# An induced-set attention with a SwiGLU network behind it: x loaded in whole rows, weights rounded in steps, strips of x in pieces on a fixed slot plan

## The chip, the cores and the metric

The kernel runs on one core of a Trainium2 chip. A core has a matrix engine (PE in the profile, with its weight loads as PEld), a vector engine (DVE), an activation engine (ACT), a general engine (POOL) and a sync engine (SP), on which this kernel issues nearly all of its DMAs in the order of its program. The metric is the device time of one execution in microseconds; lower is better. The kernel before takes 1939.54 us as the median of three runs (1937.98 to 1940.28).

## The reference

`x` is 4 batches x 12416 tokens x 128 channels, `inducing` is 32 x 128. Each batch is attended twice, and every token then goes through a gated network of width 1536:

```python
def mab(q, kv):
    s = scale * (q @ kv.transpose(0, 2, 1))
    s = s - s.max(-1, keepdims=True)
    a = np.exp(s)
    a /= a.sum(-1, keepdims=True) + 1e-09
    return a @ kv
h = mab(I, x)                # 32 inducing rows look at 12416 tokens
x = mab(x, h)                # 12416 tokens look at the 32 rows of h
rms = np.sqrt(np.mean(x * x, axis=-1, keepdims=True) + 1e-06)
xn = x / rms * rms_g
g = xn @ w_gate              # 128 -> 1536
silu = g * (1.0 / (1.0 + np.exp(-g)))
val = xn @ w_val
return (silu * val @ w_out).astype(np.float32)
```

The weights arrive as 64-bit floats and must be rounded to 32 bits on the chip; `x` is 32-bit.

## The kernel before, in words

**Tiling.** The 12416 tokens of a batch are cut into seven strips (`per` = 16, 16, 16, 16, 16, 15 and 2 tiles of 128 tokens). A strip is held in two forms: `xn`, by rows, with the tokens on the partitions, and `xT`, with the channels on them. A strip's tokens lie in four groups `q` of 32 partitions. The network works on 25 units per batch: each full strip gives four (one for each `q`), the last strip one. A unit has twelve steps `j`, one for each 128 of the width 1536; a step is called a slot here, so a batch has 300 slots, numbered 12 x unit + j.

**A slot** (`ffn`, L421). PE multiplies the stacked weights `sg` and `sv` (they hold h, the gain and w_gate or w_val together, in a high and a low half) with the unit's gathered attention weights `a` (L441, L443), ACT takes the silu (L445), DVE the product `u` (L447), and PE projects `u` with `wo` into `acc` (L431). Two or three projects are kept back in the list `late`, so PE has work while a new product is made; before the two long ACT steps (`marks`) up to five. After a unit's last project DVE transposes `acc` and SP writes it out in four DMAs (L434 to L437). In slot 2 of each unit SP is given the gather of the next unit's `a` (L417): four DMAs between partitions, for the unit of a smaller strip sixteen.

**Attention for the next batch** goes on between the slots. The steps in order: `turn_x` makes `xT` channel-wise (for batch 0 on PE with a copy on ACT or DVE, later by DVE in place, L225), `scores1` (L249), the maximum over all tokens (`max1` to `max3`), `exp1` (L273), `turn_e` and `sum_h` for h (L277, L285), `end_h`, `turn_h`, `square_h`, then `scores2` and `sub_max` per strip (L322, L330), and `exp2` (L336). `fetch(i)` reads the three rounded weight tiles back from memory (L342), and `stack(i)` multiplies them with h (L351) and lays the result into `sg` or `sv` with twelve DMAs (L358). Before, these steps are spread evenly over slots 0 to 240 of the batch ahead; `fetch(1)` follows right behind `stack(0)`. Each `sum_h` of a strip is followed by the four row loads of the batch after it (L112), and each `scores2` by the four strip loads (L118), all on SP.

**The seam** (`seam`, L369) turns a strip's attention weights into the scaled halves `hi` and `lo` that the gathers read: transposes, a square with the Gram matrix of h for the root mean square, a power on POOL, and the split (L404, L405) into halves, of which there is one buffer.

**The opening** does all of batch 0's attention before the first slot. Its rows come in 28 loads of 32 partitions, on SP and ACT in turn, and nine raw weight chunks of 512 KB are read on SP (L169) and rounded by seven DVE and two POOL operations each (L190 to L199); six are written back to memory (L203) for the later batches. At its end SP holds, in this order: the gather of unit 0, the two stacks, the strips of batch 1 once more (they were already loaded behind `scores2`), and only then the gather of unit 1.

**Buffers and queues.** At most eight DMAs are under way: each waits until the one eight places before it has landed. The pool `wp` of fetched weight tiles has three buffers, `work` three, `halves` one, `astk` (the gathered `a`) three, `up` (the products) seven.

Of the kernel before, what the change touches and what calls it, by code (L numbers as in the profile page):

```python
# [24 lines left out]
def kernel(  # L25
# [9 lines left out]
):  # L35

# [71 lines left out]
    def load_rows(b, s, queues):  # L108
        n = per[s]
        t = xnat[b, s] = xnp.tile([P, n, C], F32, name=f"xn{s}")  # L110
        for q in range(R):
            queues[q % len(queues)].dma_start(out=t[ts(q, m), :, :], in_=of(xrows, b, s)[:, ts(q, n), :])  # L112

    def load_channels(b, s):
        w = R * per[s]
        t = xT[b, s] = xtp.tile([P, w * m], F32, name=f"xT{s}")
        for k in range(R):
            nc.sync.dma_start(out=t[ts(k, m), :].rearrange("p (w c) -> p w c", c=m),  # L118
                              in_=of(xrows, b, s)[:, :, ts(k, m)])

    load_rows(0, 0, [nc.sync, nc.scalar])
# [4 lines left out]
    for s in range(1, NS):  # L126
        load_rows(0, s, [nc.sync, nc.scalar])
# [46 lines left out]
    def load_w(i, c):  # L174
# [7 lines left out]
        if wide:  # L182
            words = raw[i, c].rearrange("p (f w) -> p f w", w=2)
            low, high = words[:, :, 0], words[:, :, 1]
            e, s = (up.tile([P, 512], I32, name="u") for _ in range(2))
            f = astk.tile([P, 512], F32, name="a")
            r = outp.tile([P, 512], F32, name="o")
            fi = f.bitcast(I32)
            ve = nc.vector
            ve.tensor_scalar(out=e[:], in0=high, scalar1=20, scalar2=0x7FF, op0=ALU.logical_shift_right, op1=ALU.bitwise_and)  # L190
            ve.tensor_scalar(out=e[:], in0=e[:], scalar1=896.0, scalar2=1151.0, op0=ALU.max, op1=ALU.min)
            ve.tensor_scalar(out=e[:], in0=e[:], scalar1=-896.0, scalar2=float(1 << 23), op0=ALU.add, op1=ALU.mult)
            ve.tensor_scalar(out=s[:], in0=high, scalar1=-(1 << 31), scalar2=0x3F800000, op0=ALU.bitwise_and, op1=ALU.bitwise_or)
            ve.tensor_scalar(out=fi[:], in0=high, scalar1=12, scalar2=9, op0=ALU.logical_shift_left, op1=ALU.logical_shift_right)  # L194
            ve.tensor_tensor(out=fi[:], in0=fi[:], in1=s[:], op=ALU.bitwise_or)
            ve.scalar_tensor_tensor(out=r[:], in0=low.bitcast(U32), scalar=2.0 ** -52, in1=s.bitcast(F32)[:],  # L196
                                    op0=ALU.mult, op1=ALU.mult)
            nc.gpsimd.tensor_tensor(out=f[:], in0=f[:], in1=r[:], op=ALU.add)  # L198
            nc.gpsimd.tensor_tensor(out=dst, in0=f[:], in1=e.bitcast(F32)[:], op=ALU.mult)  # L199
        else:  # L200
            nc.sync.dma_start(out=dst if i < 2 else dst.rearrange("p (j c) -> p j c", c=C), in_=source(i, c))
        if i < 2:
            nc.sync.dma_start(out=w32[i][c][:], in_=dst)  # L203
# [3 lines left out]
    def attention(b, load_next):  # L207
# [12 lines left out]
        def turn_x(s, k):  # L220
# [9 lines left out]
            if now:  # L230
# [5 lines left out]
                if k % 4 == 3:  # L236
                    nc.vector.tensor_copy(out=dst, in_=src)
                else:
                    nc.scalar.copy(out=dst, in_=src)  # L239
# [39 lines left out]
        def sum_h(s):  # L279
# [11 lines left out]
            if load_next:  # L291
                load_rows(b + 1, s, [nc.sync])
# [53 lines left out]
        def stack(i):  # L346
# [7 lines left out]
            nc.vector.tensor_copy(out=hi[rows, :], in_=ps[rows, :])  # L354
# [262 lines left out]
```

## Time and profile before

| | us |
|---|---|
| median of three runs | 1939.54 |
| the profiled execution's own time | 1944.83 |
| its span, first to last instruction | 1943.1 |
| start of exp1 of batch 0 | 51.81 |
| first gate product of unit 0 | 157.14 |
| first gate product of unit 1 | 212.69 |
| PE busy over the span | 1722.7 |

All sums are made in the span of the profiled execution, which starts at 0. A timeline row gives start, length, engine, line, operation, the tiles written and read, and in brackets how long the engine had been idle and what ended that. "x28" at a row's end says that 28 like instructions in a row are shown as one. SPq is SP's DMA queue. The mean granted clock of PE is 0.953 of the full one.

### The profile page before, as it was taken

How to read it: one execution, taken by the hardware profiler on the slowest of the kernel's cores; microseconds unless marked ns; L12 is line 12 of the kernel's file. 1: busy time of each engine (PE TensorE's matmuls, PEld its weight loads, DVE VectorE, ACT ScalarE, POOL GpSimd, SP SyncE). 2: the span in 40 equal slices, each digit the busy share in tenths (PEclk: the TensorE clock that was granted, in tenths of full speed). 3: DMA queues.
4: the chain of work that ended last, by engine and by line, in shares of the span. 5: the costliest groups of instructions: out<-in, count | busy, mean ns of one | idle time of the engine just before them, and what ended most of it. 6: DMA issues, size and time to landing. Idle time of an engine off the chain costs nothing.

```text
span 1943.1 us, 20398 instructions
## 1 busy us (share of the span) xinstructions
PE 1722.7 (89%) x6258; PEld 959.7 (49%) x6258; DVE 1156.7 (60%) x2010; ACT 751.2 (39%) x1246; POOL 176.9 (9%) x137
## 2 busy tenths in 40 slices
PE   4413699999897999999989899999999899999998
PEld 3201355555454655555545555555555555555555
DVE  1824476666555667566646577666666465656654
ACT  2001244433343443533344344443354344444443
POOL 0321101101101001101101011001011011001100
PEclk9756799999999999999989899999999899999999
DMA  7797411165721111155741111111221111111111
GB/s 186 170 167 126 72 31 29 36 142 104 142 43 29 30 33 33 28 116 109 139 73 32 24 31 33 38 23 44 63 45 33 24 31 33 33 33 33 33 32 26
DMA packets 443197, 120.41 MB, mean 62 GB/s; under 512 B 418736, under 2 KB 422864, under 8 KB 440528
## 3 DMA queue, kind: packets, MB, share of 16 engines
q1 hardware_dynamic: 442224, 115.91, 30.3%
q10 hardware_dynamic: 864, 3.20, 0.7%
q8 instruction: 50, 0.82, 0.2%
q14 instruction: 59, 0.48, 0.1%
HBM read 60.31 MB, written 27.00 MB: 45 GB/s over the span
## 4 chain that ended last, share of the span: by engine, by line
PE 80%; SPq 9%; DMA 5%; ACT 2%; DVE 2%; issue 1%; DVEq 0%; ACTq 0%
PE acc L431 48%; PE gv L441 13%; PE gv L443 13%; SPq L118 5%; SPq L417 3%; DMA xn<-in_x_dram 2%; PE mm L245 2%; DMA a<-lo 1%; PE mm L285 1%; DVE u L447 1%; PE mm L385 1%; PE gv L233 1%; ACT silu L445 1%; SPq L358 0%; SPq L436 0%
## 5 line engine op out<-in xcount | busy, mean ns | idle before, releaser
L431 PE MATMUL acc<-u,wo 128*128 128x512 f32 (+2 forms) x2400 | 1212.9, 588 | 62.3 <-DVE u L447 62.2
L447 DVE TENSOR_TENSOR u<-silu,gv 128x512 f32<-128x512 f32 (+2 forms) x1200 | 796.9, 670 | 598.5 <-ACT silu L445 590.5
L445 ACT ACTIVATE silu<-gv 128x512 f32<-128x512 f32 (+2 forms) x1200 | 700.2, 585 | 1080.1 <-PE gv L441 590.5
L441 PE MATMUL gv<-a,sg 128*128 128x512 f32 (+2 forms) x1200 | 929.9, 775 | 83.7 <-DVE a L194 49.5
L431 PEld LDWEIGHTS acc<-u,wo 128*128 128x128 f32 x2400 | 443.2, 190 | 217.8 <-DVE u L447 77.9
L443 PE MATMUL gv<-a,sv 128*128 128x512 f32 (+2 forms) x1200 | 469.0, 391 | 10.0 <-DMA sv<-wlo 6.7
L441 PEld LDWEIGHTS gv<-a,sg 128*128 128x128 f32 x1200 | 229.0, 191 | 367.0 <-issue 294.6
L443 PEld LDWEIGHTS gv<-a,sv 128*128 128x128 f32 x1200 | 229.8, 191 | 284.6 <-issue 195.6
L388 POOL TENSOR_TENSOR z<-z,sc 128x512 f32<-128x512 f32 (+2 forms) x28 | 31.8, 1136 | 1276.5 <-DVE z L387 1134.6
L396 POOL TENSOR_TENSOR rs<-ms,mhalf 128x16 f32<-128x16 f32 (+2 forms) x28 | 71.8, 2564 | 97.2 <-DVE ms L394 97.1
L434 DVE STREAM_TRANSPOSE o<-acc 128x512 f32<-128x512 f32 (+2 forms) x100 | 69.2, 692 | 1.6 <-PE acc L431 1.1
L225 DVE STREAM_TRANSPOSE xT<-xT 128x512 f32<-128x512 f32 (+2 forms) x84 | 53.2, 633 | 0.0
L404 DVE CAST hi<-aT 128x512 fp32r<-128x512 f32 (+2 forms) x28 | 11.0, 392 | 69.4 <-DMA a<-hi 69.3
L331 POOL TENSOR_TENSOR sc<-sc,mx 128x512 f32<-128x512 f32 (+2 forms) x24 | 22.5, 936 | 220.6 <-ACT silu L445 114.2
L336 ACT ACTIVATE sc<-sc 128x3104 f32<-128x3104 f32 (+2 forms) x5 | 11.4, 2274 | 55.7 <-POOL sc L331 34.5
L233 PE MATMUL gv<-ident,xn 128*128 128x128 f32 x97 | 15.8, 326 | 17.1 <-ACT xT L239 16.4
L385 PE MATMUL mm<-eT,gram 128*128 128x512 f32 (+2 forms) x56 | 26.0, 545 | 0.5 <-DVE eT L376 0.5
L398 POOL TENSOR_TENSOR sc<-sc,rs 128x512 f32<-128x512 f32 (+2 forms) x28 | 26.1, 933 | 2.2
L355 DVE TENSOR_TENSOR wlo<-gv,whi 96x512 fp32r<-96x512 f32 x2 | 1.4, 686 | 39.8 <-DMA sg<-whi 39.8
L233 PEld LDWEIGHTS gv<-ident,xn 128*128 128x128 f32 x97 | 13.4, 169 | 22.9 <-ACT xT L239 20.1
L405 DVE TENSOR_TENSOR lo<-aT,hi 128x512 fp32r<-128x512 f32 (+2 forms) x28 | 17.4, 621 | 11.6 <-DMA a<-lo 11.3
L198 POOL TENSOR_TENSOR a<-a,o 128x512 f32<-128x512 f32 x9 | 11.7, 1303 | 119.0 <-DVE o L196 119.0
(122 smaller groups left out, 466.5 us busy)
## 6 DMA issues: line engine op xcount, KB each, us to landing
xT<-in_x_dram SPq DMA_DIRECT2D x80, 256.0 KB, 5.1
out_dram<-o SPq DMA_DIRECT2D x320, 64.0 KB, 2.0
xn<-in_x_dram SPq DMA_DIRECT2D x70, 256.0 KB, 5.4
a<-hi SPq DMA_DIRECT2D x160, 64.0 KB, 2.0
a<-lo SPq DMA_DIRECT2D x160, 64.0 KB, 2.0
w<-w SPq DMA_DIRECT2D x21, 256.0 KB, 3.1
xT<-in_x_dram SPq DMA_DIRECT2D x16, 240.0 KB, 4.8
out_dram<-o SPq DMA_DIRECT2D x64, 60.0 KB, 2.0
```

Source lines behind the costliest of these rows:

```text
L118: nc.sync.dma_start(out=t[ts(k, m), :].rearrange("p (w c) -> p w c", c=m), in_=of(xrows, b, s)[:, :, ts(k, m)])
L225: nc.vector.transpose(out=t[:, ts(k, n * m)], in_=t[:, ts(k, n * m)])
L233: nc.tensor.transpose(ps[:, ts(t - k * R, P)], xnat[b, s][:, t, :], ident[:])
L385: nc.tensor.matmul(ps[:, 0:n * m], gram[b][:], st["eT"][:], start=True, stop=True)
L396: nc.gpsimd.tensor_tensor(out=rs[:, 0:n], in0=ms[:, 0:n], in1=mhalf[:, 0:n], op=ALU.pow)
L417: nc.sync.dma_start(out=a[ts(k, m), ts(q, w)].bitcast(F32), in_=half[ts(q0 + q, m), 0:w].bitcast(F32))
L431: nc.tensor.matmul(acc[:, 0:T], wo[:, j, :], t[:, 0:T], start=(j == 0), stop=(j == NJ - 1))
L434: nc.vector.transpose(out=o[:, 0:T], in_=acc[:, 0:T])
L441: nc.tensor.matmul(g[:, 0:T], sg[:, ts(j, P)], a[:, 0:T], start=True, stop=True)
L443: nc.tensor.matmul(v[:, 0:T], sv[:, ts(j, P)], a[:, 0:T], start=True, stop=True)
L445: nc.scalar.activation(sl[:, 0:T], g[:, 0:T], AF.Silu)
L447: nc.vector.tensor_tensor(out=t[:, 0:T], in0=sl[:, 0:T], in1=v[:, 0:T], op=ALU.mult)
```

## The change

It does six things.

1. Batch 0's rows come in seven loads of 128 partitions, a strip each, all on SP, with the first three raw weight chunks in between; in this batch a strip's tokens lie in the order (q i t) instead of (i q t), in the output too. ACT makes all the copies into `xT`.
2. The rounding of a chunk is cut into six steps, which are called between other steps: three after each `scores1`, six after `exp1`, six after `square_h`, six inside the first seam, twelve after the gather of unit 0, and the rest in slots 0 to 3. The scaling of the exponent moves from DVE to POOL, except for chunk (1, 2), which is rounded on DVE alone. A new raw chunk is read after one has been put away.
3. `scores2` no longer loads strips. The strips of batch 1 are loaded once: four pieces (one of 32 channels each) at the end of the opening, the others one in every fourth slot. Those of batches 2 and 3 come one in every sixth slot, from slot 215 of the batch before.
4. In batch 0, `scores2` and `sub_max` of strips 1 to 6 and the rest of `exp2` move from the opening into slots 1 to 22.
5. The even spread is replaced by fixed slots: `turn_x` from 20, `scores1` from 36, the maximum at 126 to 130, `exp1` at 134, `turn_e` and `sum_h` from 140, `fetch(0)` at 170, `fetch(1)` at 178, `end_h` at 184, `stack(0)` at 191, `scores2` from 194, `stack(1)` at 198, `exp2` at 254.
6. Each group q is written out by itself, so the last unit of a batch has sixteen small output DMAs instead of four. In the first seam of batch 0 two POOL multiplications are on DVE; the second seam is a unit later; batch 0's `stack` casts on ACT.

The core of the diff:

```diff
     def of(dram, b, s):
-        return dram[ds(b * N + start[s], P * per[s]), :].rearrange("(i w) c -> i w c", i=m)
+        d = dram[ds(b * N + start[s], P * per[s]), :]
+        return d.rearrange("(i q t) c -> q i t c" if b else "(q i t) c -> q i t c", q=R, i=m)
...
-    def load_rows(b, s, queues):
+    def load_rows(b, s):
         n = per[s]
         t = xnat[b, s] = xnp.tile([P, n, C], F32, name=f"xn{s}")
-        for q in range(R):
-            queues[q % len(queues)].dma_start(out=t[ts(q, m), :, :], in_=of(xrows, b, s)[:, ts(q, n), :])
+        if b:
+            for q in range(R):
+                nc.sync.dma_start(out=t[ts(q, m), :, :], in_=of(xrows, b, s)[q])
+        else:
+            nc.sync.dma_start(out=t[:], in_=xrows[ds(start[s], P * n), :].rearrange("(p t) c -> p t c", t=n))
...
+        ge = ve if (i, c) == (1, NC - 1) else nc.gpsimd
+        return [
+            lambda: ve.tensor_scalar(out=e[:], in0=high, scalar1=20, scalar2=0x7FF,
+                                     op0=ALU.logical_shift_right, op1=ALU.bitwise_and),
...
         def scores2(s):
             nc.vector.transpose(out=sc[b][:, cols[s]], in_=scores(s, st["hT"][:, 0:m]))
-            if load_next:
-                load_channels(b + 1, s)
...
-                for k in range(R):
-                    nc.sync.dma_start(out=of(out, b, s)[:, ds(q0 * per[s], nb), ts(k, m)],
-                                      in_=o[ts(k, m), 0:T].rearrange("p (w c) -> p w c", c=m))
+                w = per[s] * m
+                for q in range(nq):
+                    for k in range(R):
+                        nc.sync.dma_start(out=of(out, b, s)[q0 + q][:, :, ts(k, m)],
+                                          in_=o[ts(k, m), ts(q, w)].rearrange("p (t c) -> p t c", c=m))
...
+    for s in range(NS):
+        load_rows(0, s)
+        if reads and s < NC:
+            fetch_raw(*reads.pop(0))
...
         if s:
             f["scores1"](s - 1)
+            convert(6 * NC // (NS - 1))
...
-    convert()
-    convert()
+    convert(6)
...
+    f["fetch"](0)
+    convert(6)
+    turn_a, square, scale, apply, split = seam(0, 0)
+    turn_a()
+    f["stack"](0)
+    square()
+    convert(3)
+    scale()
+    convert(3)
+    f["fetch"](1)
+    f["stack"](1)
+    apply()
+    split()
     gather(0, 0)
-    for i in range(2):
-        f["fetch"](i)
-        f["stack"](i)
-    while queue:
-        convert()
+    convert(12)
+    pieces = {b: [(b, s, k) for s in range(NS) for k in range(R)] for b in range(1, B)}
     if B > 1:
-        for s in range(NS):
-            load_channels(1, s)
+        for _ in range(R):
+            load_channels(*pieces[1].pop(0))
...
+        if not b:
+            for k in range(4):
+                add(k, convert, 3)
+            for s in range(1, NS):
+                add(3 * s - 2, f["scores2"], s)
+                add(3 * s, f["sub_max"], s)
+            add(3 * NS + 1, f["exp2"], 1, NS)
+            marks.append(3 * NS + 1)
+        if b + 1 < B:
+            g = attention(b + 1, b + 2 < B)
+            for k, one in enumerate(pieces[b + 1]):
+                add(4 * k if not b else 6 * k, load_channels, *one)
...
+                add(140 + 6 * s, g["turn_e"], s)
+                add(144 + 6 * s, g["sum_h"], s)
+                add(194 + 8 * s, g["scores2"], s)
...
+            for i in range(2):
+                add(170 + 8 * i, g["fetch"], i)
+                add(191 + 7 * i, g["stack"], i)
+            add(254, g["exp2"], 0, NS)
+            marks += [134, 254]
+        if b + 2 < B:
+            for k in range(215, NU * NJ, 6):
+                add(k, load_channels, *pieces[b + 2].pop(0))
```

Below are two places in SP's order. The first is the end of the opening. Names: `xT` are strips and `xn` rows of batch 1, `w` with a source is a rounded chunk on its way to memory, `a` is the gather, `sg` and `sv` are the stacks. Before:

```order
L118 DMA xT_733<-in_x_dram 32x64x32 x4
L203 DMA w_155<-silu 128x512
L118 DMA xT_762<-in_x_dram 32x60x32 x4
L118 DMA xT_783<-in_x_dram 32x8x32 x4
L417 DMA a<-hi 32x512
L417 DMA a<-lo 32x512
...
L358 DMA sg<-whi 32x512 x6
L358 DMA sg<-wlo 32x512 x6
L358 DMA sv<-whi 32x512 x6
L358 DMA sv<-wlo 32x512 x6
L118 DMA xT_882<-in_x_dram 32x64x32 x4
L118 DMA xT_887<-in_x_dram 32x64x32 x4
```

After:

```order
L115 DMA xn_586<-in_x_dram 32x1920 x4
L115 DMA xn_595<-in_x_dram 32x256 x4
L188 DMA w_119<-silu 128x512
L371 DMA sg<-whi 32x512 x6
L371 DMA sg<-wlo 32x512 x6
L188 DMA w_120<-silu 128x512
L371 DMA sv<-whi 32x512 x6
L371 DMA sv<-wlo 32x512 x6
L434 DMA a<-hi 32x512
L434 DMA a<-lo 32x512
...
L124 DMA xT_758<-in_x_dram 32x64x32 x4
```

The strips ahead of the gather and those behind the stacks are gone but for four pieces; the row loads stand directly ahead of the stacks, and the gather of unit 0 has moved behind them.

The second place is SP around the second weight fetch in a later batch's attention, with the semaphores that each DMA waits for (DMAHW is a DMA eight places before; PE, DVE an engine). Names: `w_...` from `w1...` is the second fetch, `a_...` the gather. After:

```order
L352 DMA w_2871<-w02_117 128x512 [waits DMAHW2_49]
L434 DMA a_2875<-hi_2249 32x512 [waits DMAHW3_49]
...
L115 DMA xn5_2939<-in_x_dram 32x1920 [waits DMAHW7_49,PE_49]
...
L352 DMA w_2982<-w10_118 128x512 [waits DMAHW3_49,PE_49]
L352 DMA w_2983<-w11_119 128x512 [waits DMAHW4_49,PE_49]
L352 DMA w_2984<-w12_120 128x512 [waits DMAHW5_49,PE_49]
L115 DMA xn6_3011<-in_x_dram 32x256 [waits DMAHW6_49]
...
L455 DMA out_0_dram<-o_3026 512x1x32 [waits DMAHW2_49,DVE_49]
...
L434 DMA a_3040<-hi_2900 32x512 [waits DMAHW6_49]
...
L371 DMA sg_3096<-whi_3153 32x512 [waits DMAHW2_49,DVE_49]
```

Before, the second fetch:

```order
L358 DMA sg_2987<-whi_3367 32x512 [waits DMAHW0_49,DVE_49]
...
L358 DMA sg_2987<-wlo_3368 32x512 [waits DMAHW6_49,DVE_49]
...
L342 DMA w_3411<-w10_153 128x512 [waits DMAHW4_49,PE_49]
...
L436 DMA out_0_dram<-o_3418 32x16x32 [waits DMAHW7_49,DVE_49]
...
L417 DMA a_3438<-hi_3000 32x512 [waits DMAHW3_49]
```

On PE, the product that frees the first fetch's tiles stands in the change at slot 191, and the gate product of the next unit, which reads the gather `a_3040`, two places behind it:

```order
L361 MATMUL mm_3149<-w_2869,hg_3092 32x512 [waits DMAHW0_49]
L361 MATMUL mm_3149<-w_2870,hg_3092 32x512 [waits DMAHW1_49]
L361 MATMUL mm_3149<-w_2871,hg_3092 32x512 [waits DMAHW2_49]
L448 MATMUL acc_2998<-u_3129,wo_112 128x512
L460 MATMUL gv_3171<-a_3040,sg_615 128x512 [waits DMAHW6_49,DMAHW1_49,DMAHW7_49,DMAHW0_49,Activation_49]
```

The second fetch now stands ahead of the stack DMAs of the first product, with four small row loads, an output and a gather between them; before, it stood behind them.

More of the change, by code (lines that the diff above doesn't have):

```diff
@@ L454, with convert @@
     f = attention(0, B > 1)
[L455 to L464 removed]
+    reads = chunks[:len(places)]
+    unread = chunks[len(places):]
+    for s in range(NS):
+        load_rows(0, s)
+        if reads and s < NC:
+            fetch_raw(*reads.pop(0))
+    for one in reads:
+        fetch_raw(*one)
+    queue, steps = list(chunks), []
+    def convert(n):
+        for _ in range(n):
+            if not steps and queue:
+                steps.extend(load_w(*queue.pop(0)))
+            if steps:
+                steps.pop(0)()
     f["open_"]()
@@ L487 @@
     f["square_h"]()
-    chain = seam(0, 0)
-    for s in range(1, NS):
-        f["scores2"](s)
-        f["sub_max"](s)
-        if s % 2 and chain:
-            chain.pop(0)()
-        if len(queue) > NC:
-            convert()
-    for k in chain:
-        k()
-    f["exp2"](1, NS)
-    while len(queue) > NC:
-        convert()
-    gather(0, 0)
-    for i in range(2):
-        f["fetch"](i)
-        f["stack"](i)
-    while queue:
-        convert()
+    f["fetch"](0)
+    convert(6)
+    turn_a, square, scale, apply, split = seam(0, 0)
@@ L543, in schedule, with add @@
-        last = units.index((full - 1, 0, 1)) * NJ
-        at = [last * k // len(steps) for k in range(len(steps))]
-        plan = {}
-        for k, step in zip(at, steps):
-            plan.setdefault(k, []).append(step)
-        return plan, [at[k] for k in marks]
+        plan, marks = {}, []
+        def add(k, step, *args):
+            plan.setdefault(int(k), []).append(lambda: step(*args))
+        if not b:
[6 more added lines that the diff above has]
+            marks.append(3 * NS + 1)
```

141 lines of the change are left out of this document (59 added, 82 removed).

## The prediction

> **What bounds the kernel now.** I read the page first, its chain of waits and its 40 slices:
>
> ```profile
> PE 80%; SPq 9%; DMA 5%; ACT 2%; DVE 2%; issue 1%; DVEq 0%; ACTq 0%
> PE   4413699999897999999989899999999899999998
> ```
>
> PE carries 80% of the chain, but SP's queue and the DMAs carry 14%. The slices show where: PE is 40% busy or less in the first four (49 us each), and nearly full afterwards. So the opening is bound by transfers, the rest by PE. The windows from the second unit of batch 0 to the end put numbers on the rest (columns: window, length, busy of PE, PEld, DVE, ACT, POOL, granted clock, DMA share, GB/s):
>
> ```profile
> 213.50:647.30 433.80, 411.30 (x1493) 226.06 (x1493) 270.24 (x474) 178.68 (x295) 38.05 (x28) 0.98 0.34 66
> 647.30:1096.90 449.60, 426.89 (x1541) 235.39 (x1541) 280.45 (x490) 185.85 (x307) 38.01 (x28) 0.98 0.33 64
> 1096.90:1534.10 437.20, 423.69 (x1541) 233.95 (x1541) 280.50 (x490) 185.88 (x308) 38.03 (x28) 0.99 0.18 37
> 1534.10:1943.10 409.00, 393.50 (x1215) 226.97 (x1213) 240.01 (x392) 175.35 (x300) 27.15 (x18) 0.99 0.17 31
> ```
>
> PE idles 22.5, 22.7, 13.5 and 15.5 us in them (length less busy). The gain has to come from the 213 us ahead of them, and a loss from new idle time in them.
>
> **Part 1, to the first softmax.** The windows and the opening's timeline (start, length, engine, line; the last two rows are the page's DMA issues, with KB and us to landing):
>
> ```profile
> 0.00:30.00 30.00, 5.00 (x21) 4.17 (x21) 2.05 (x10) 0.14 (x1) 0.76 (x7) 1.00 0.96 210
> 32.00:36.00 4.00, 4.00 (x20) 2.42 (x19) 0.69 (x1) 2.29 (x5) 0.00 (x0) 1.00 1.03 394
> 64.00:93.00 29.00, 17.41 (x211) 8.14 (x203) 23.54 (x49) 0.63 (x1) 8.58 (x8) 0.79 1.01 231
> 29.86 1.28 ACT L239 ACT_TABLE_LOAD   x1 [29.86 <-DMA xn<-in_x_dram]
> 39.14 1.97 PE L233 MATMUL gv<-ident,xn 128*128 128x128 f32 x16
> 42.03 1.97 PE L233 MATMUL gv<-ident,xn 128*128 128x128 f32 x16
> 51.81 2.88 ACT L273 ACTIVATE sc<-sc,nbias 128x3104 f32<-128x3104 f32 x1 [3.25 <-DVE nbias L269]
> 52.14 0.43 DVE L191 TENSOR_SCALAR u<-u 128x512 int32<-128x512 int32 x1
> 55.40 1.37 DVE L191 TENSOR_SCALAR u<-u 128x512 int32<-128x512 int32 x1
> w<-w SPq DMA_DIRECT2D x21, 256.0 KB, 3.1
> a<-lo SPq DMA_DIRECT2D x160, 64.0 KB, 2.0
> ```
>
> Batch 0's x (6.36 MB) moves at 210 GB/s with the DMA engines 96% busy: 32 partitions per load set that rate, and the same form gives 231 again at 64 to 93. Raw weights into 128 partitions move at 394. ACT issues half the loads and cannot copy before 29.86. Afterwards x and three raw chunks (1.57 MB) come in 128-partition loads: 7.93 MB at 394 GB/s is 20.1 us, and about 3 until the last lands (the `w<-w` row), so 23. A strip costs PE and ACT 2.89 us (39.14 to 42.03); two are left when the last lands, 5.8. The rounding steps put between the scores delay DVE by up to 3 x 0.94 = 2.8 (the same step took 0.43 once and 1.37 three us later); the chain of the maximum takes 2. So exp1 starts at 34, not 51.81. Bounds: 28 if neither strips nor rounding lag (23 + 2.9 + 2), 49 if the loads stay at 210 (37.8 + 3 + the same tail).
>
> The Trainium skill ("DMA: Bandwidth & Descriptors", section "Where 436 GB/s comes from") lets HBM give a core about 358 GB/s; by that the loads would take 22.2 us and the sum be 2 us longer, an estimate by that page. The trace's 394 GB/s, over 4 us only, disagrees.
>
> **Part 2, from there to the second unit.**
>
> ```profile
> 57.91 0.33 SPq L203 DMA_DIRECT2D w<-w  x1
> 60.94 8.88 PE L285 MATMUL gv<-xn,e 128*32 128x128 f32 x194 [9.36 <-DVE e L277]
> 63.76 29.23 SPq L112 DMA_DIRECT2D xn<-in_x_dram  x28
> 93.82 14.18 SPq L118 DMA_DIRECT2D xT<-in_x_dram  x8
> 149.16 3.71 SPq L358 DMA_DIRECT2D sg<-whi  x6
> 157.14 0.76 PE L441 MATMUL gv<-a,sg 128*128 128x512 f32 x1 [49.46 <-DVE a L194]
> 164.32 44.35 SPq L118 DMA_DIRECT2D xT<-in_x_dram  x28
> 210.63 0.59 SPq L417 DMA_DIRECT2D a<-lo  x1
> 212.69 0.76 PE L441 MATMUL gv<-a,sg 128*128 128x512 f32 x1 [28.60 <-DMA a<-lo]
> ```
>
> SP is the path from 63.76 on: 28 row loads for batch 1 (29.23), then 28 strip loads among the spills (93.82 to 146), gather and 24 stack copies (4 x 3.71), then the same 28 strips once more (44.35), behind which unit 1's gather stands. That gather ends unit 0 at 212.69, though its own work is some 20 us. The change takes both sets of strips off this queue; four pieces stay. What stays is SP's 28 row loads, since each strip's rows are replaced as sum_h frees them.
>
> One rounded chunk instead of two stands between exp1 and turn_e, so the first row load comes 7.5 us after exp1's start instead of 12: at 41.5. Then 29.2 of row loads, 3 until the eighth DMA back has landed, 14.8 for the stacks, 1 for two spills (0.33 each if nothing holds them), 2.5 for the gather and 2 for its landing: the first gate at 94, not 157.14. DVE's work in that time (three chunks' steps at 0.4 to 1.4 us, scores2 of strip 0, the seam) lets the first stack be ready at about 62 and the second at 72 to 75; SP comes to them at 74 and 82. So it is hidden, with some 7 us to spare; DVE being later than that would add the difference.
>
> Unit 0 now also holds four of the scores2 steps and the last rounding. The chain in the steady state prices a slot and a block of scores (start, us, what):
>
> ```profile
> 495.52 0.99 PE mm L351 x6
> 499.35 0.86 PE acc L431 x2
> 500.67 0.86 PE acc L431 x2
> 504.62 0.99 PE mm L245 x8
> 552.37 2.70 ACT sc L336
> ```
>
> A slot is 500.67 - 499.35 = 1.32. Twelve are 15.8, four scores 4.0, and I allow 4 for the low clock at the start and DVE's queue: 24. Unit 1 starts at 118 instead of 212.69: **-95 us** (bounds: 28 or 49 for exp1 and 20 or 28 for the unit give -105 and -76).
>
> **Part 3, the steady state.** Its stalls before, in batch 0's seventeenth to twenty-third units:
>
> ```profile
> 516.42 12.53 SPq L118 DMA_DIRECT2D xT<-in_x_dram  x8
> 535.43 0.41 DVE L404 CAST hi<-aT 128x480 fp32r<-128x480 f32 x1 [9.83 <-DMA a<-hi]
> 537.41 2.07 PE L431 MATMUL acc<-u,wo 128*128 128x512 f32 x2 [9.11 <-DVE u L447]
> 630.30 1.97 PE L431 MATMUL acc<-u,wo 128*128 128x480 f32 x2 [8.97 <-DVE u L447]
> 640.63 1.94 SPq L436 DMA_DIRECT2D out_dram<-o  x4
> 646.81 0.47 PE L441 MATMUL gv<-a,sg 128*128 128x512 f32 x1 [0.26 <-DMA a<-lo]
> 509.36 2.11 SPq L342 DMA_DIRECT2D w<-w  x3
> 1930.52 10.08 SPq L436 DMA_DIRECT2D out_dram<-o  x8
> ```
>
> Eight strips in one go (12.53) hold back a gather; DVE's split waits for it 9.83 and PE 9.11. The same happens in batch 1, not in batch 2, which loads no strips. With one strip in four or six slots (1.57 us of SP in 5 to 8) I let both go: -9 each. The stall of 8.97 is of another kind (sixteen small gathers of one unit, then the split that waits for them), and stays.
>
> **The new wait.** The weight tiles have three buffers. Before, the second weight fetch stood behind the first stack product; now it is issued at slot 178 and can't start before the product of slot 191 frees the tiles. SP works in order: behind it stand four small row loads, an output of four DMAs, and the gather of the unit that starts at slot 192. From the product on, SP needs 2.1 (three fetches) + 1.5 (four row loads of 32 KB, by the shortest issue, 0.33, a little over) + 1.9 (output) + 2.4 (four gathers at 0.59) + 2.0 of landing = 9.9, while PE has two stack products and one project left, 1.7. PE so stands **8.2** at the start of that unit in batches 0 and 1, and 6.7 in batch 2, which has no row loads. Floor 0 if the tiles come free earlier than the order says, ceiling 13 if the stalled SP also holds the next gather.
>
> Other terms: two scores2 in unit 1 of batch 0, 2 x 0.99, less what fills gaps: +1.4; exp2 among the units takes ACT away for 2.7 and two table loads of 1.28, of which the queue of ready products covers a part: +3.5. Sixteen output DMAs instead of four at the end of each batch (12 x 0.485, from 1.94 for four): at the end of batches 0 to 2 they delay the next batch's second gather by 5.8, of which about 5 is covered: +1 each in batches 1 to 3; at the very end they stand bare: +5.8.
>
> Sum: -95; batch 0 -9 + 1.4 + 3.5 + 8.2 = +4; batch 1 -9 + 8.2 + 1 = 0; batch 2 6.7 + 1 = +8; batch 3 1 + 5.8 = +7. Net **-75** (-95 + 19, rounded). The profiled execution, 1944.83 us with a span of 1943.1, would come to 1869 with a span of 1867. It lies 5.3 above the median of the runs, 1939.54, so the median comes to **1864**.
>
> **Rivals.** (a) The fetch's wait costs nothing, because gathers are needed later than I count. For it: before, a gather that landed at the last moment cost PE only 0.26 (646.81), so a little slack more would do. Against: the order on SP and the three tiles leave no slack, since product, fetch and gather follow each other. Time: 1864 - 23 = 1841. (b) Whole rows stay at 210 GB/s, HBM being the limit and not the 32 partitions: exp1 at 49, 1864 + 15 = 1879. Against it stand 394 GB/s in the same queue. The Trainium skill ("SBUF — State Buffer", section "Door 1: The DMA port swizzle") says that 32 partitions reach half of the ports and 128 all of them; 210 beside 394 agrees. (c) Strips in pieces still hold up the gathers, since each may have to wait for the DMA eight places back: both 9 us stalls stay, 1864 + 18 = 1882. For it: eight strips took 12.53 us with no more traffic than this. (d) Slower than before: SP never makes up for its wait at the fetch, and every gather of units 16 to 24 comes as late as the first. 27 stalls of 8.2 are 221, of which 23 are counted: 2062. It decides from about ten further stalls on (75 / 8.2). For it: SP's work there is 7.4 of stack copies, 3.1 of strips, 4.3 of output and gather in a unit of 17. Against: of PE's 22.5 us idle in batch 0 the two stalls of 9.11 and 8.97 are 18, so no units behind a late gather lost much again.
>
> **The numbers.** Forecast 0.64, (a) 0.13, (b) 0.11, (c) 0.09, (d) 0.03. The forecast's own range is 1854 (the lower bound of -105) to 1878 (the fetch's ceiling of 13 in three batches; slow loads are rival (b)); with (a), (b) and (c) I take 1840 to 1884. A measurement tells about 0.2% (4 us) from no change. Only (d) is slower, and 0.01 is left for a gain that vanishes: faster 0.96, same 0.01, slower 0.03.
>
> **What would show it.** Whole rows: DMA near 390 GB/s in the first 20 us and exp1 at 28 to 38. SP: one block of 28 row loads, then the stacks, the first gate near 94, unit 1 near 118. Fetch: in three batches a gap of 7 to 8 us of PE before the gate of unit 16, released by a gather, and SP's second `w` fetch starting right after the stack product. No 9 us stall at the nineteenth unit. It would be wrong if the first gate came after 110, or if gathers kept landing late in units 17 to 24.

## The result and the profile after

The changed kernel takes **1888.74 us** as the median of four runs (1883.78 to 1892.92), against 1938.76 us of the kernel before. The ratio is 0.974, with a 95% interval of 0.9714 to 0.9767. The forecast was 1864 with a range of 1840 to 1884: faster it is, but by 50 us instead of 75, and the time lies above the range. The profiled execution took 1892.92 us with a span of 1891.1.

PE's row of the 40 slices and the chain of waits on the changed kernel's page, the answer to the two rows that the prediction began with:

```profile
PE   6199999989979999998997999998998999999997
...
PE 82%; DMA 5%; SPq 5%; DVE 3%; ACT 2%; issue 2%; POOL 0%; DVEq 0%; ACTq 0%
```

SP's queue has 5% of the chain instead of 9%, and two slices of the opening are thin instead of four. So the gain came where it was expected. The windows show what happened afterwards. First the loads, then batches 0 to 3 from unit 1 (batch 0) or unit 0 to their end; columns as before:

```profile
0.00:22.00 22.00, 15.09 (x98) 11.56 (x99) 6.21 (x22) 10.32 (x18) 3.01 (x10) 1.00 0.90 357
118.40:567.40 449.00, 418.61 (x1509) 228.04 (x1508) 273.40 (x483) 183.26 (x298) 40.33 (x31) 0.97 0.34 67
567.40:1020.70 453.30, 425.83 (x1541) 234.44 (x1541) 280.14 (x490) 185.75 (x308) 37.95 (x28) 0.98 0.33 64
1020.70:1473.20 452.50, 428.72 (x1541) 235.90 (x1540) 280.24 (x490) 185.68 (x307) 37.96 (x28) 0.98 0.22 42
1473.20:1891.10 417.90, 396.77 (x1215) 228.90 (x1214) 239.90 (x392) 175.24 (x300) 27.14 (x18) 0.98 0.16 31
```

Against 433.8, 449.6, 437.2 and 409.0 the batches are 15.2, 3.7, 15.3 and 8.9 us longer, 43 in all, where the prediction allowed 19. Of the 43, PE's idle time (length less busy) is 29, and its busy time 14, though it does only two scores2 steps more (16 products in the first window). The granted clock fell from 0.98, 0.98, 0.99, 0.99 to 0.97, 0.98, 0.98, 0.98.

The opening, from the timeline, came out as worked out:

```profile
34.13 2.88 ACT L285 ACTIVATE sc<-sc,nbias 128x3104 f32<-128x3104 f32 x1 [6.55 <-DVE nbias L281]
...
42.44 30.00 SPq L115 DMA_DIRECT2D xn<-in_x_dram  x28
...
73.98 3.77 SPq L371 DMA_DIRECT2D sg<-whi  x6
...
86.37 3.70 SPq L371 DMA_DIRECT2D sv<-wlo  x6
...
94.12 0.77 PE L460 MATMUL gv<-a,sg 128*128 128x512 f32 x1 [26.36 <-DMA a<-lo]
...
117.58 0.79 PE L460 MATMUL gv<-a,sg 128*128 128x512 f32 x1
```

exp1 starts at 34.13, the row loads at 42.44, the first gate at 94.12, and the last row, unit 1's first gate, at 117.58, against 34, 41.5, 94 and 118.

The rest of the time is in three units of each batch. From the first silu of one unit to the first of the next, the fifteenth, sixteenth and seventeenth unit (slots 168 to 203) took 17.5 + 19.4 + 18.2 = 55.2 us in every batch before. After, they took 72.8, 68.7 and 69.7: **45.5 us more** in the three batches, where 23.1 were allowed. The timeline there, in batch 0:

```profile
355.04 2.62 SPq L455 DMA_DIRECT2D out_dram<-o  x4
357.70 2.10 SPq L352 DMA_DIRECT2D w<-w  x3
...
363.71 0.43 DVE L421 CAST hi<-aT 128x512 fp32r<-128x512 f32 x1 [4.74 <-DMA a<-hi]
...
365.51 2.07 PE L448 MATMUL acc<-u,wo 128*128 128x512 f32 x2 [3.13 <-DVE u L466]
...
390.59 1.29 SPq L352 DMA_DIRECT2D w<-w  x3
391.93 1.81 SPq L115 DMA_DIRECT2D xn<-in_x_dram  x4
393.85 2.62 SPq L455 DMA_DIRECT2D out_dram<-o  x4
396.51 0.62 SPq L434 DMA_DIRECT2D a<-hi  x1
...
400.62 0.77 PE L460 MATMUL gv<-a,sg 128*128 128x512 f32 x1 [9.00 <-DMA a<-lo]
```

And two windows, behind each of the two gaps in it:

```profile
365.50:369.50 4.00, 3.99 (x7) 2.17 (x8) 2.17 (x5) 0.60 (x1) 0.00 (x0) 0.59 0.54 115
400.60:406.70 6.10, 6.08 (x14) 3.24 (x18) 1.95 (x3) 1.39 (x3) 0.00 (x0) 0.53 0.37 91
```

Three things are seen. The predicted stall is there, in the predicted order (fetch, row loads, output, gather), with 9.00 us; in batches 1 and 2 it is 8.20 and 6.56. Behind it PE runs 6.1 us at a granted clock of 0.53. And there is a stall of 3.13 in the fifteenth unit that nobody expected: an output and the first fetch stand ahead of that unit's gather on SP, the gather lands late, DVE's split waits 4.74 for it (it may not overwrite the halves before the gather has read them), and PE waits behind DVE.

### The profile page after: what moved, and what is told of

The parts are those of the page before. It is cut to its first block, busy times and chain, and to the rows that moved or that the text cites. A ratio compares the mean times of both kernels' runs of the same rounds, so it can differ in the third digit from the quotient of the medians.

```text
span 1891.1 us, 20393 instructions
## 1 busy us (share of the span) xinstructions
PE 1731.8 (92%) x6258; PEld 961.9 (51%) x6258; DVE 1141.6 (60%) x1998; ACT 757.4 (40%) x1256; POOL 176.8 (9%) x141
## 4 chain that ended last, share of the span: by engine, by line
PE 82%; DMA 5%; SPq 5%; DVE 3%; ACT 2%; issue 2%; POOL 0%; DVEq 0%; ACTq 0%
PE acc L448 50%; PE gv L460 14%; PE gv L462 13%; SPq L434 3%; DMA xn<-in_x_dram 2%; DMA a<-lo 2%; PE mm L257 2%; DVE u L466 1%; PE mm L398 1%; DMA a<-hi 1%; PE mm L297 1%; ACT silu L464 1%; SPq L455 1%; PE gv L257 0%; ACT sc L285 0%
## 5 line engine op out<-in xcount | busy, mean ns | idle before, releaser
L448 PE MATMUL acc<-u,wo 128*128 128x512 f32 (+2 forms) x2400 | 1220.9, 592 | 58.5 <-DVE u L466 58.2
L414 POOL TENSOR_TENSOR sc<-sc,rs 128x512 f32<-128x512 f32 (+2 forms) x27 | 25.1, 928 | 2.1
L464 ACT ACT_TABLE_LOAD x8 | 10.3, 1283 | 26.7 <-PE gv L460 26.6
L297 PE MATMUL mm<-xn,e 128*32 128x128 f32 x582 | 20.7, 276 | 0.0
L400 DVE STREAM_TRANSPOSE z<-mm 128x512 f32<-128x512 f32 (+2 forms) x28 | 17.9, 639 | 3.5 <-PE mm L398 3.5
L257 PE MATMUL mm<-xT,indT 128*32 128x512 f32 (+2 forms) x168 | 20.0, 547 | 0.0
L257 PE MATMUL mm<-xT,hT 128*32 128x512 f32 (+2 forms) x168 | 20.0, 547 | 0.0
```

The lines of the kernel that those rows point to most:

```text
L257: nc.tensor.matmul(ps[ts(q, m), 0:w], lhsT, xT[b, s][:, ts(q, w)], start=True, stop=True)
L297: nc.tensor.matmul(ps[ts(t % R, m), 0:C], e[:, ts(t, m)], xn[:, t, :], start=t < R, stop=t + R >= n)
L448: nc.tensor.matmul(acc[:, 0:T], wo[:, j, :], t[:, 0:T], start=(j == 0), stop=(j == NJ - 1))
L464: nc.scalar.activation(sl[:, 0:T], g[:, 0:T], AF.Silu)
```

## The experiments

Ratios are to runs of the kernel before that were timed beside each run, with 95% intervals; the changed kernel has 0.974. A difference of ratios is turned into us with the 1938.76 of the kernel before. The changed kernel's own runs spread over 9 us, so that differences of less than some 10 us are read from the traces, unit by unit.

### The second fetch behind the product that frees its tiles

```diff
                 nc.tensor.matmul(ps[ts(c, m), :], st["hg"][:], w[:], start=True, stop=True)
+            if b and not i:
+                fetch(1)
...
-                add(170 + 8 * i, g["fetch"], i)
+                if not i:
+                    add(170, g["fetch"], i)
```

> The changed kernel with the second weight fetch issued on SP directly behind the three stack products of slot 191, ahead of the stack's own DMAs, instead of at slot 178. Theory A (the fetch waits for the product and holds the gather of the seventeenth unit; the three gaps of 9.0, 8.2 and 6.6 us cost besides some 3 us each because the granted clock is 0.53 for the 6 us that follow): about 24 + 9 = 33 us less than the changed kernel's 1889, 1856, and no gap over 3 us at the seventeenth unit. Theory B (only the idle time itself counts): 24 us less, 1865. Theory C (SP is too full there in any order, so the gather of the next unit is late instead): within 10 us of 1889, with a new gap of 5 us or more at the start of the eighteenth unit.

Measured: 1862.57 us, ratio 0.9568 (0.9548 to 0.9589). That is 0.017 below the changed kernel, 33 us by the ratio; the profiled span falls by 27.5. Batch 0 from unit 1 on and its seventeenth unit, in windows:

```profile
117.60:557.00 439.40, 417.81 (x1512) 227.94 (x1511) 273.38 (x482) 184.00 (x299) 40.35 (x31) 0.97 0.35 68
391.50:411.00 19.50, 19.50 (x75) 9.03 (x69) 13.93 (x21) 6.57 (x11) 0.00 (x0) 1.00 0.53 125
```

In the second row PE is busy all through, at full clock. The sixteenth unit is 18.14 us in all three batches (27.69, 26.88 and 25.23 in the changed kernel), the seventeenth 19.43 (21.86, 20.68, 21.41). Together that is 25.4 and 5.7 us. The stall in the fifteenth unit stays and is 3.1 us longer in all (25.5, 24.1 and 20.8 against 23.2, 21.1 and 23.0), which is why the span shows less than the 31 of these units. So the fetch's wait with its low clock is worth 27 to 33 us, not the 23.1 of the forecast. The units show theory A; the times of the whole kernel alone would hardly tell it from B.

### Two buffers of the halves

```diff
-    halves = pool("halves", 1)
+    halves = pool("halves", 2)
```

> The changed kernel with two buffers of hi and lo instead of one. Theory A (the gaps in front of the project, which DVE's product releases, all come from the split, which may not overwrite the one pair of halves before the last gather has read it): the three gaps of 9.6, 8.9 and 8.8 us of the twenty-fourth unit, the three of 2.6 to 3.1 of the fifteenth and the small ones of 1 to 3 go, 56 us of gaps together, and with them some 10 us of low clock: 1889 - 60 = 1829. Theory B (only the long gaps are the split's; in the fifteenth unit it is the first fetch and the row loads ahead of the gather): 27 us of gaps and 6 of clock less, 1856. Theory C (the sixteen small gathers hold SP and the next gather whatever the buffers): within 5 us of 1889.

Measured: 1821.43 us, ratio 0.9357 (0.9336 to 0.9377): 0.038, about 75 us below the changed kernel, more than theory A's 60. The view of waits (idle us, how often, the longest), two rows of the changed kernel:

```profile
PE acc L448 <- DVE u L466: 58.2, 22, 9.5
...
PE gv L460 <- DMA a<-lo: 57.1, 8, 26.4
```

and of this one:

```profile
PE gv L460 <- DMA a<-lo: 61.9, 13, 23.2
...
DVE u L466 <- PE acc L448: 5.5, 6, 2.0
```

PE's 22 waits on DVE's product, 58.2 us, have no row of their own any more; its waits for gathers stay. So those stalls were DVE standing in the split, which must not overwrite the one pair of halves before late gathers have read it. The twenty-fourth unit fell from 26.7, 26.4 and 26.9 to 17.5, 17.0 and 17.7. The fifteenth fell from 23.21, 21.13 and 23.02 to 18.25, 18.23 and 18.25: its stall, with the low clock behind it, was 12.6 us in three batches.

### The kernel before, without its second loading of the strips

```diff
     while queue:
         convert()
-    if B > 1:
-        for s in range(NS):
-            load_channels(1, s)
```

> The kernel before, without the second loading of batch 1's strips at the end of the opening (28 DMAs); nothing else is changed, the output is the same. Theory A (those 44.35 us of SP hold the gather of unit 1, and nothing else does): unit 1's gate comes when unit 0 is done, some 20 us behind 157.1, at 177 to 180 instead of 212.7: 1939 - 34 = 1905, two thirds of what the whole change gains. Theory B (DVE's rounding of the last three chunks limits unit 0 to much more than 20 us): 1920 or above.

Measured: 1917.18 us, ratio 0.985 (0.9826 to 0.9874), 29 us faster than the kernel before. Three gate products of the timeline: unit 0's first, its last, and unit 1's first:

```profile
158.24 0.77 PE L441 MATMUL gv<-a,sg 128*128 128x512 f32 x1 [50.44 <-DVE a L194]
...
183.72 0.80 PE L441 MATMUL gv<-a,sg 128*128 128x512 f32 x1
...
185.05 0.79 PE L441 MATMUL gv<-a,sg 128*128 128x512 f32 x1
```

Unit 1 starts at 185.05 instead of 212.69. Unit 0 needs 27 us: PE waits 6.66 in it for the last stack copies, and 2.69 for a product that DVE makes only after its rounding. Theory A is right in its cause and 5 us too high in its size. This one deletion alone gains more than half of what the whole change gains.

### Rows in 32-partition loads

```diff
-            nc.sync.dma_start(out=t[:], in_=xrows[ds(start[s], P * n), :].rearrange("(p t) c -> p t c", t=n))
+            for q in range(R):
+                nc.sync.dma_start(out=t[ts(q, m), :, :], in_=of(xrows, b, s)[q])
```

> The changed kernel, with batch 0's rows in 28 loads of 32 partitions on SP, the same 8 KB per partition, the raw chunks in between as before. Theory A (32 partitions set the rate of about 220 GB/s, and whole rows raise it): the last strip lands at 37 to 40 instead of 23, exp1 starts at 47 to 50 instead of 34.1, and all that follows on SP shifts: 1889 + 14 = 1903. Theory B (HBM or the number of DMAs sets the rate): below 1893.

Measured: 1904.93 us, ratio 0.979 (0.9767 to 0.9813), 10 us more than the changed kernel. exp1 in the timeline:

```profile
44.91 2.88 ACT L286 ACTIVATE sc<-sc,nbias 128x3104 f32<-128x3104 f32 x1 [5.32 <-DVE nbias L282]
```

and the window of the loads:

```profile
0.00:22.00 22.00, 10.79 (x54) 8.31 (x55) 3.16 (x14) 6.64 (x11) 1.00 (x8) 1.00 0.93 232
```

232 GB/s against 357 at like busy shares (0.93 and 0.90); without the start, from 3 to 20 us, it is 241 against 401. In the changed kernel itself the rows of batch 1, which come in 32 partitions, show the slow rate too:

```profile
42.50:72.50 30.00, 12.33 (x125) 4.65 (x125) 18.80 (x46) 1.68 (x3) 6.33 (x4) 0.70 1.00 224
```

So theory A holds. The edit also makes 28 loads of seven, but the number and size of the loads are not what sets the rate: in the changed kernel's trace the weight fetches, 256 KB a DMA like these row loads but into 128 partitions, move their 2 KB packets in 84 ns (median, 390.5 to 394 us), about 390 GB/s over 16 engines, while a packet of 8 KB into 32 partitions takes 598 (42 to 50 us), 219 GB/s. The last strip lands at 36.8 instead of 23.3, close to what was expected. exp1 comes only 10.8 us later, and the first silu 9.3, because the copies and scores lag less behind slower loads: exp1 starts 8.1 us after the last landing instead of 10.9. That is where the expected 14 was too high. The Trainium skill ("SBUF — State Buffer", section "Door 1: The DMA port swizzle") has 32 partitions reach half the ports; here they keep 65% of the rate (232 of 357), the raw chunks into 128 partitions being in both figures.

### PE kept busy during the stall

```diff
+    def fill():
+        ps = ps_m.tile([P, 512], F32, name="mm", tag="mm")
+        for _ in range(15):
+            nc.tensor.matmul(ps[:], ident[:], wo.rearrange("p j c -> p (j c)")[:, 0:512], start=True, stop=True)
...
                 add(191 + 7 * i, g["stack"], i)
+            add(191, fill)
```

> The changed kernel with fifteen extra products of 128x512 on PE (ident against a piece of wo, into a bank that nothing reads) between the first stack product and the gate of the seventeenth unit, in three batches: some 6.5 us of otherwise useless work inside each gap of 9.0, 8.2 and 6.6 us. Theory A (the low clock behind a gap comes from PE having been idle): PE runs on at full clock after it, the seventeenth unit is some 2.5 us shorter three times, 8 us less than the changed kernel, at a ratio to before of 0.970 against 0.974. Theory B (the clock falls there for another reason, or the slow products are slowed by the stack copies): no change, or up to 2 us more.

Measured: 1894.58 us, ratio 0.9745 (0.9729 to 0.9761). The extra products took twice what I had put down, and ran past the gap (timeline):

```profile
388.09 13.14 PE L536 MATMUL mm<-wo,ident 128*128 128x512 f32 x30
```

The window behind them:

```profile
401.00:408.00 7.00, 7.00 (x27) 3.31 (x26) 3.35 (x5) 2.28 (x4) 0.00 (x0) 1.00 0.37 83
```

The sixteenth unit grew to 31.0, but the granted clock behind it is 1.00 and the seventeenth unit 19.43 in all three batches. By its time the run decides nothing; by its clock it speaks for theory A. The same edit with `range(7)` stays inside the gap:

> As the fifth experiment, with seven extra products instead of fifteen: one turned out to take 0.86 us, so fifteen were 12.9 us and longer than the gap; seven are 6.0 us, inside the gaps of 9.0, 8.2 and 6.6. Theory A (low clock after idleness): the seventeenth unit starts when it did and takes 19.4 instead of 21.9, 20.7 and 21.4, so 5 to 6 us less than the changed kernel in all, ratio 0.971. Theory B: ratio 0.974 and the seventeenth unit as in the changed kernel.

Measured: 1884.78 us, ratio 0.9685 (0.9671 to 0.9699). Two windows behind the gap, in batch 0 and in batch 1:

```profile
397.50:405.00 7.50, 5.61 (x22) 2.78 (x23) 3.35 (x5) 1.79 (x3) 0.00 (x0) 1.00 0.38 92
861.40:869.00 7.60, 7.60 (x23) 3.65 (x24) 3.44 (x5) 2.13 (x4) 0.00 (x0) 0.78 0.44 102
```

The sixteenth units kept their length (27.4, 26.7, 25.1), the seventeenth took 19.42, 21.09 and 19.43. Useless work in the gap made the work behind it faster in two batches of three, by 2.4 and 2.0 us; in batch 1 the clock fell all the same, behind a remaining gap of 2.30, while it did not in batch 0 behind one of 2.99. So the low clock follows from idle time, but not by the length of the gap alone. Where the gap lies decides. The clock records of each of the twelve traces change between 1.00 and 0.50 only, and only at multiples of 3.41 us from one another. Such windows around the two gaps, two in batch 0 and two in batch 1:

```profile
394.66:398.08 3.42, 1.74 (x5) 0.43 (x3) 0.00 (x0) 0.00 (x0) 0.00 (x0) 1.00 0.57 109
398.08:401.49 3.41, 2.10 (x7) 1.43 (x8) 0.69 (x1) 0.87 (x2) 0.00 (x0) 1.00 0.42 102
...
858.88:862.29 3.41, 1.11 (x4) 0.67 (x4) 0.00 (x0) 0.45 (x1) 0.00 (x0) 1.00 0.41 97
862.29:865.70 3.41, 3.41 (x7) 1.67 (x5) 1.38 (x2) 0.74 (x2) 0.00 (x0) 0.50 0.45 109
```

The gap of 2.99 is cut in two by a window's end and leaves PE idle for 1.68 and 1.31 of 3.41 us; the clock stays. The gap of 2.30 lies in one window, and the next window gets 0.50. Behind the first 100 us of the twelve traces each of the 104 windows at full clock with more than 1.97 us of idle PE was followed by one at half clock, and none of those with less than 1.87; the clock came back only behind a window with at most 0.50 us idle. The Trainium skill ("TensorE: Matmul & The Clock Gate", section "What's actually happening") speaks of a free-running window of about 3.4 us after which an idle array gets half its pulses: the 3.41 and the 0.50 agree with that, but here the window need not be idle throughout. In time the run is 0.0055 better than the changed kernel; the units in question explain 4 us of those 11, and the rest lies within the spread of its runs.

### The first fetch behind the gather

```diff
-                add(170 + 8 * i, g["fetch"], i)
+                add(171 + 7 * i, g["fetch"], i)
```

> The changed kernel with the first weight fetch one slot later (171 instead of 170), which puts it behind the gather of the sixteenth unit on SP instead of ahead of it. Theory A (those 2.1 us ahead of the gather make the split late and PE stand 2.6 to 3.1 us in the fifteenth unit, with 1.5 us of low clock): the fifteenth unit falls from 23.2, 21.1 and 23.0 to about 19, 9 to 11 us less in all. Theory B (the row loads and outputs ahead of it do): under 4 us less.

Measured: 1878.76 us, ratio 0.9658 (0.9634 to 0.9683). The fifteenth unit falls to 20.10, 19.40 and 18.54, 9.3 us less in three batches: theory A. The profiled span is 10 us shorter; that the medians show 16 is again within the spread. In the six other variants that leave this place as it is, the fifteenth units of the three batches sum to 68.8 to 71.8 us, against 67.4 in the changed kernel and 58.0 here, so 9.3 is not too high. What is left in batches 0 and 1 (1.9 and 1.2 above 18.25) was not tested; an output of 2.62 and 1.96 us still stands directly ahead of the gather there.

### Eight strips in one go

```diff
-            for k in range(215, NU * NJ, 6):
+            for k in [217] * 8 + list(range(263, NU * NJ, 6)):
                 add(k, load_channels, *pieces[b + 2].pop(0))
```

> The changed kernel with eight of the fifteen strip pieces that are loaded from slot 215 on issued together in slot 217, ahead of the gather of the twentieth unit, in batches 0 and 1; the other seven stay in every sixth slot from 263. Theory A (eight strips in one go take 12.5 us of SP, the gather is late, the split waits for it, and PE behind it): the nineteenth unit grows from 19.3 and 18.4 to 27 to 28, as in the kernel before, 18 us more in all than the changed kernel. Theory B (that stall went away for another reason): within 4 us of it.

Measured: 1896.01 us, ratio 0.975 (0.973 to 0.9771). The nineteenth unit grew only by 3.1 and 1.5 us (22.37 and 19.95), not by 8 to 9, and the ratio is within 2 us of the changed kernel's. Theory A fails in its size, and theory B's range holds. The timeline, SP's rows and the split:

```profile
427.50 0.59 SPq L434 DMA_DIRECT2D a<-hi  x1
428.14 0.59 SPq L434 DMA_DIRECT2D a<-lo  x1
428.82 13.04 SPq L124 DMA_DIRECT2D xT<-in_x_dram  x8
441.96 3.85 SPq L455 DMA_DIRECT2D out_dram<-o  x4
...
449.26 0.41 DVE L421 CAST hi<-aT 128x480 fp32r<-128x480 f32 x1 [2.56 <-DMA a<-hi]
```

The burst takes 13.04 us, about as before (12.53). But SP had nothing else to do and began it at 428.8, nearly ten us before the nineteenth unit (438.31) in whose slot 1 it is written. It ran ahead of the program's slots, and only the last part of the burst was in the way. In the kernel before, the timeline of SP shows why it could not:

```profile
500.06 5.40 SPq L358 DMA_DIRECT2D sg<-whi  x6
505.56 3.70 SPq L358 DMA_DIRECT2D sg<-wlo  x6
509.36 2.11 SPq L342 DMA_DIRECT2D w<-w  x3
...
529.05 3.00 SPq L436 DMA_DIRECT2D out_dram<-o  x4
532.10 0.54 SPq L417 DMA_DIRECT2D a<-hi  x1
```

There SP works without a break from 500.06 on: the stack's copies, the fetch, an output, a gather, the eight strips (516.42), and only then the output and the gather. By these rows it was the queue ahead of the burst that made it late. So the plan's keeping strips away from the stack has a part in the cure, beside the small pieces; how much each of the two does alone in the kernel before was not tested.

### Four output DMAs instead of sixteen

```diff
+                if b and nq > 1:
+                    whole = out[ds(b * N + start[s], P * per[s]), :].rearrange("(i w) c -> i w c", i=m)
+                    for k in range(R):
+                        nc.sync.dma_start(out=whole[:, :, ts(k, m)],
+                                          in_=o[ts(k, m), 0:T].rearrange("p (w c) -> p w c", c=m))
+                    return
```

> The changed kernel with the last unit of batches 1 to 3 written out in four DMAs instead of sixteen (batch 0 keeps its sixteen, since its tokens lie in another order). Theory A (the forecast's prices: 5.8 us at the very end, 1 for each of the two batches whose second gather they delay): 8 us less than the changed kernel, ratio 0.970. Theory B (the last writes overlap with what follows): within 2 us.

Measured: 1883.88 us, ratio 0.9685 (0.9671 to 0.9698). The end of SP's queue in the changed kernel (four of these twenty belong to the unit before the last), then in this one:

```profile
1873.58 15.51 SPq L455 DMA_DIRECT2D out_dram<-o  x20
```

```profile
1874.52 2.57 SPq L456 DMA_DIRECT2D out_dram<-o  x4
```

The last unit with its end falls from 21.27 to 15.08: 6.2 us, with 5.8 expected. At the start of batches 2 and 3 it brings only 0.4 and 0. Theory A for the end; the other two microseconds of its 8 are not there. The ratio is 11 us lower; what these units do not show of that lies within the spread of the runs.

### Together

The second fetch, the halves and the four outputs as above, and batch 1's row loads taken out of the opening (the part of the edit that is new):

```diff
-            if load_next:
+            if load_next and b:
                 load_rows(b + 1, s)
...
             marks.append(3 * NS + 1)
+            if B > 1:
+                for s in range(NS):
+                    add(99 + 6 * s, load_rows, 1, s)
```

> Four edits to the changed kernel together: the second fetch behind the product (as in the first experiment), two buffers of hi and lo (as in the second), the last unit of batches 1 to 3 written out in four DMAs instead of sixteen, and batch 1's row loads in slots 99 to 135 of batch 0 instead of in the opening, ahead of the stacks. If the effects add: 1889 - 34 - 68 - 9 (6 at the end, 3 at the start of batch 1's last gather) - 15 (the first gate at about 79, when DVE has the second stack ready, instead of 94) = 1763, ratio 0.909. If the row loads only move their wait: about 1778.

Measured: **1769.8 us** (1768.42 to 1771.7), ratio 0.91 (0.9086 to 0.9115). The page's slices and chain:

```profile
PE   5499999999999999999999999999999999999998
...
PE 90%; SPq 2%; ACT 2%; DVE 2%; DMA 2%; issue 1%; DVEq 0%; ACTq 0%
```

and a window from unit 1 of batch 0 into batch 1:

```profile
106.80:555.00 448.20, 439.24 (x1602) 242.03 (x1601) 293.71 (x516) 197.00 (x321) 41.61 (x32) 1.00 0.44 87
```

The effects add nearly as expected (1763). PE is at nine tenths or more from the third slice to the last but one, and the granted clock in that window is 1.00. The first silu comes at 84.5 instead of 96.3, a gain of 11.7 where 15 were hoped for: with the row loads gone, SP waits 18.7 us, to 60.43, for a chunk that POOL is still rounding, then 1.5 for ACT's cast of the second stack, and ends its stack copies at 78.

## Why the prediction was wrong

- **Part 1 and part 2, right.** The sum of -95 for the time to unit 1 came out as -95.1 (117.58 against 212.69), and its steps did too, to within 1 us each. The rate was right as well: the 357 GB/s over the first 22 us hold the start, whose first 3 us move less than 100 GB/s; from 3 to 20 us it was 401, and the last strip came at 23.3. The Trainium skill ("DMA: Bandwidth & Descriptors", section "Where 436 GB/s comes from") gives some 358 as HBM's limit for one core; the trace does not agree, with 401 over 17 us, and the measurement decides. The run with rows in 32 partitions confirms why whole rows are faster, with 10 us in place of the 15 of rival (b). One slack was misjudged without harm: the second stack was ready at 79.9, not at 72 to 75, since DVE waited 13.41 us until copies of the first stack had landed; SP came to it at 82.6, so some 3 us were to spare and not 7.
- **The strips, right in what goes, wrong in why.** The nineteenth unit lost its stall, -8.3 and -9.8 for -9 each. The step gave the small pieces as the whole cure; the burst in one go cost only 3.1 and 1.5, so the cure lies also in what no longer stands ahead of it on SP.
- **The new wait, right in its place and length.** 9.00, 8.20 and 6.56 for 8.2, 8.2 and 6.7, with the releaser that was named.
- **What failed is the price of that stretch.** The step reads: "PE so stands 8.2 at the start of that unit in batches 0 and 1, and 6.7 in batch 2", and the sum takes those 23.1 for all that happens there: it put the low clock behind the stall, and the place of the first fetch, at nothing. The fifteenth to seventeenth units lost 45.5. Of these 23.8 are the three stalls. 5.7 are the low clock behind them, by the seventeenth unit with the stall and without it. 12.6 are the stall of the fifteenth unit with its clock, by the run with two halves. Of the last 3.5, 1.9 is work that the new plan has moved into these three units (18.25 + 18.14 + 19.43 = 55.8 without stalls, against 55.2, three times), and 1.6 lies in the sixteenth unit beside its gap (25.4 against 23.8). The 22.4 missing there are nearly the whole error of 24 (a span of 1891.1 against 1867). Both causes could be read in advance: the prediction quoted a project of 2.07 us behind the old stall, without asking why it took twice the 1.02 that two projects take elsewhere in the timeline, and the order shown ahead of it has the first fetch directly ahead of a gather, which the sum does not count.
- **The end, right**: 6.1 for 5.8.
- **Small terms, partly luck.** The +1.4 and +3.5 of batch 0 did not show: its second and third unit take 35.4 us together, 35.7 before. The +1 for the start of batch 1 was 3.1, those of batches 2 and 3 were 0.4 and 0. These and other small differences nearly cancel, so that the net error of 24 lies so close to the 22.4 by luck. Two bounds do not follow from their own terms: exp1 with slow loads comes at about 52 (37.8 + 3 + 11), not 49, and a fetch ceiling of 13 in three batches gives 1880, not 1878.
- **Rivals.** (a), that the fetch costs nothing, is refuted by the run with the second fetch behind the product: without the wait the sixteenth and seventeenth units are 31 us shorter. (c), gathers late as before at the nineteenth unit, did not come about, although its kind of stall did, four units earlier. (d), a backlog that is never made up, did not: the eighteenth unit is at its length again (18.1 in batches 0 to 2).

## What to carry over

An engine that issues all DMAs in order is a resource with a timetable of its own: for each transfer that the compute waits for, list what stands ahead of it on that engine and what that work itself waits for, and put a fetch that has to wait for a buffer behind the product that frees the buffer. A stall of the matrix engine can cost more than its length, here 1.3 to 2.4 us more in the next unit for each of 7 to 9, since the clock comes back only behind a window of 3.41 us in which PE was busy. And before a slot plan is tuned, look for work done twice and for a single buffer between a late reader and the next writer: the one deletion gave 29 us and the second buffer about 75, more than the whole rewritten plan.

## What the runs showed that was not expected

The output of a unit costs SP 2.62 us in batch 0 of the changed kernel and 1.96 in batch 3, for the same four DMAs and bytes: in batch 0's token order its pattern has become 512x1x32, elsewhere it is 32x16x32. An output stands ahead of the gather of each unit, so this takes 0.7 us of SP there, and the stall is 9.00 in batch 0 against 8.20 in batch 1. That the pattern is the cause was not tested by itself.
